# Zero products ahead of TensorE's first work, one pair by product instead of two, fills moved, and weight loads issued a slot earlier, in an attention and hard-swish kernel

## The chip, the cores and the metric

The kernel runs on one core of a Trainium2 chip. The metric is device time in microseconds (us) of one execution. The profile is of one such execution, and times in it count from its start. TensorE (PE, with its weight loads PEld), VectorE (DVE), ScalarE (ACT), GpSimd (POOL) and SyncE (SP) each run their own list of instructions in order and wait for each other on semaphores; transfers go through queues that SP, ACT and POOL feed.

## The reference

Attention over 8 batches of 8 heads, with 576 positions and 64 columns a head, then a two-layer network over all 4608 tokens:

```python
scores = matmul(q, k.T) / 8
cum = cumsum(maximum(s, 0))
scores = where(causal, -1e9, scores + minimum(-(cum[i] - cum[j]), 0))
attn = softmax(scores)
x = (attn @ v)                    # heads side by side: 4608 x 512
h = x @ w_in                      # 512 -> 2048
out = (h * clip(h + 3, 0, 6) / 6) @ w_out   # 2048 -> 512
```

The bias `cum[j] - cum[i]` is a product of rows: the kernel gets it inside the score product by giving q and k a few more rows.

## The kernel before

**Pairs.** The 64 heads are worked as 32 pairs, p = 0 to 31; four pairs (`PPB`) are one batch. For a pair, q and k come in as float32, are cast to float16 tokens `tok`, transposed by TensorE into `qk` (64 rows for the numbers, rows 64 to 67 for the bias), and v is cast into `va`, whose columns 64 and 65 hold ones so that the product with P also gives the sum of the softmax. Each head has three score banks (`scores(p, hh, 0..2)`, then one `corner` a pair), an exponential on ACT into `P`, and fifteen products with `va` (`av`, line 372). `norm` divides, and `transpose_x` puts the pair's result into `xT`, which the network reads.

**The bias.** `load_aug` (line 137) copies rows of the running sum into rows 64 to 67 of `qk` by DMA. In the first pairs, `p < NROW` (two of them before), this copy would come late; there rows 64 to 67 are filled with zeros, and the bias comes by separate products of 128 rows (`by_rows`, line 268, and line 313) from `rows_of` and `picked`, a masked copy of the sums for each head (line 622).

**The front.** `s` is loaded, DVE takes its running sum (lines 593 to 619: scale, scan, and four steps that split it in float16 parts), ACT casts the first pair's tokens, PE transposes them (line 219), and DVE and ACT copy the transposes into `qk` (line 205). Before the running sum DVE works through a row of fills (lines 567 to 589).

**The order by hand.** All instructions stand in an order written out in the loop over p. For p below 4 only attention runs. From p = 4 on `group()` puts a piece of the network between the steps of attention, by turns four products of the first layer (`m1`, line 438, into `ph`) and four of the second (`m2`, line 465, into `po`); pieces become due by counts, whatever the data's arrival, so PE meets a late weight by standing still. Up to p = 8 only the first batch's pieces are due, so these slots have fewer of them.

**Loads.** SP issues v and, for the first four pairs and from pair 9, q and k (lines 114, 125, 129). POOL issues the tokens of pairs 4 to 8 with a cast on the way (line 109), the bias rows, and the weights: `w_in` in four pieces (I0 to I3, line 145), `w_out` in eight (U0 to U7, line 153), each in the slot of the pair that `weights_in` names. Being in order, POOL issues none of them while it waits: it casts q, k and v, and `load_aug` waits there until PE has done the scores that still read the rows to be overwritten.

Of the kernel before, what the change touches and what calls it, by code (L numbers as in the profile page):

```python
# [9 lines left out]
F32 = mybir.dt.float32  # L10
F16 = mybir.dt.float16
# [7 lines left out]
def kernel(  # L19
# [10 lines left out]
    nc = tc.nc  # L30

    B, H, SEQ, D = q.shape
# [5 lines left out]
    NP = NHEADS // 2  # L38
    PPB = H // 2
# [5 lines left out]
    NQK = 3  # L45
    NRAW = 3
    VW = 66
    NROW = 2

# [16 lines left out]
    def keep(name, shape, dt, n=1):  # L68
        made = [
            cpool.tile(shape, dt, name=f"{name}{i}", tag=f"{name}{i}") for i in range(n)  # L70
        ]
        return made if n > 1 else made[0]
# [17 lines left out]
    bias3 = keep("bias3", [128, 1], F32)  # L90
    rows_of = keep("rows_of", [128, 2, 640], F16, 2)
    sel = keep("sel", [128, 4], F32)
    picked = keep("picked", [128, 4, SEQ], F16)

# [24 lines left out]
    def load_v(p, eng):  # L121
        b, h0 = p // PPB, 2 * (p % PPB)
        vraw = vraws[p % NRAW]
        for hh in range(2):
            eng.dma_start(
                out=vraw[:, hh, 0:4, :],
                in_=v[b, h0 + hh, 0:512, :].rearrange("(t p) d -> p t d", p=128),
            )
        eng.dma_start(
            out=vraw[0:64, :, 4, :],  # L130
            in_=v[b, h0 : h0 + 2, 512:SEQ, :].rearrange("h p d -> p h d"),
        )
# [27 lines left out]
    def fill(eng, ap, value):  # L160

        word = np.array([value, value], np.float16).view(np.float32)[0]
        eng.memset(ap.bitcast(F32), float(word))  # L163

    def init_va(i, eng):


        fill(eng, vas[i][:, :, 0:4, 64:66], 1.0)
        fill(eng, vas[i][0:64, :, 4, 64:66], 1.0)
        fill(eng, vas[i][64:128, :, 4, :], 0.0)  # L170
# [41 lines left out]
    def transpose(p, i, copies=(nc.vector.tensor_copy, nc.vector.tensor_copy)):  # L212
        tok, qk = toks[p], qks[p % NQK]
        pt = t_bank(i == 1, "pt")
        if flat(p):
            for c in range(5):
                w = 128 if c < 4 else 64
                c0 = 9 * D * i + 128 * c
                nc.tensor.transpose(  # L219
                    pt[0:w, 128 * c : 128 * (c + 1)], tok[:, c0 : c0 + w], ident  # L220
                )
            order(qk, i, pt.rearrange("p (t c) -> p t c", c=128), 0, copies)
            return
        for hh in range(2):
            for c in range(3):
                n = 96 * (3 * hh + c)
                nc.tensor.transpose(
                    pt[:, n : n + 96],
                    tok[:, i, hh, 2 * c : 2 * c + 2, :].rearrange("p e d -> p (e d)"),
                    ident[0:96, 0:96],  # L230
                )
        on_act = i == 1 and p % 2 == 0
        copies = (nc.scalar.copy if i else nc.vector.tensor_copy,
                  nc.scalar.copy if on_act else nc.vector.tensor_copy)
        for par in range(2):
            to = qk[0:64, 0, i, par : par + SEQ]
            copies[par](
                out=bass.AP(
                    to.tensor,
                    to.offset,  # L240
                    [list(to.ap[0]), [2 * SPAD + 64, 2], [6, 96], [2, 3]],
                ),
                in_=pt[64 * par : 64 * par + 64, 0:SEQ].rearrange(
                    "p (h c t) -> p h t c", h=2, c=3
                ),
            )
# [282 lines left out]
    for p in (1, 2):  # L529
        for i in range(2):  # L530
            load_qk(p, i)
        load_v(p - 1, nc.sync)
    fill(nc.gpsimd, ident, 0.0)
    nc.gpsimd.affine_select(
        out=ident,
# [21 lines left out]
    def set_stair(i, copy):  # L557
        for hh in range(2):
# [4 lines left out]
                in_=stair_sb[64:128, :, None, :].to_broadcast([64, 2, 5, 128]),  # L563
            )

    ones = work.tile([128, SEQ], F32, tag="ones", bufs=1)
    nc.vector.memset(ones, 1.0)
    nc.vector.memset(bias3, 3.0)
    fill(nc.gpsimd, rows_of[0][:, 0, :], 1.0)
    fill(nc.gpsimd, rows_of[0][:, 1, SEQ:640], 0.0)  # L570
    for i in range(NROW):
        fill(nc.vector, qks[i][64:68, :, :, :], 0.0)
    for i in range(NQK):
        init_va(i, nc.gpsimd)
    for i in range(NQK):
        for hh in range(2):
            r = SEQ + 64 * hh
# [43 lines left out]
    def pick(g):  # L621
        nc.vector.tensor_scalar(
            out=picked[:, g, :],
            in0=rows_of[0][:, 0, 0:SEQ],
            scalar1=sel[:, g : g + 1],
            scalar2=None,
            op0=ALU.mult,
        )
# [13 lines left out]
    pick(0)  # L642
    transpose(0, 0)
    transpose(0, 1, (nc.scalar.copy,) * 2)
    for g in range(1, 2 * NROW):
        pick(g)
    cast_qk(1)
    cast_v(0)
    load_aug(2, nc.sync)
    cast_qk(2)  # L650
    for i in range(2):
        load_qk(4, i)
    cast_v(1)
    nc.sync.dma_start(out=stair_sb, in_=stair_dram.ap())


    I, U = load_w_in, load_w_out
    weights_in = {
        3: ((I, 1),),
        4: ((U, 0), (U, 1)),  # L660
        5: ((I, 2), (U, 2)),
        6: ((U, 3), (I, 3)),
        7: ((U, 4), (U, 5)),
        8: ((U, 6), (U, 7)),
    }
    for p in range(NP):
        nxt = p + 1 < NP
        if p + 3 < NP:
            load_v(p + 3, nc.sync)
        if NPE <= p + 4 < NP:  # L670
            for i in range(2):
                load_qk(p + 4, i)
        if p == 2:
            load_w_in(0)
        if PPB <= p < PPB + 3:
            set_stair((p + 1) % NQK, nc.gpsimd.tensor_copy)
            load_aug(p + 1, nc.gpsimd)
        if p and p < NP - 2 and not PPB <= p + 1 < PPB + 3:
            load_aug(p + 2, nc.gpsimd)
        c = p + 2  # L680
        if p and c < NP and flat(c):
            cast_qk(c)
            if c >= NPE:
                crossbar_qk(c)
        if p and nxt:
            cast_v(p + 1)
        for fn, c in weights_in.get(p, ()):
            fn(c)
        if 2 <= p and p + 3 < NPE:
            for i in range(2):  # L690
                load_qk(p + 3, i)
        if p == 10:
            load_s(1, (nc.sync,) * 4)
            fill(nc.gpsimd, rows_of[1][:, 0, :], 1.0)
        if p == 11:
            cum1(1, nc.gpsimd)
        if p == 12:
            cum2(1)
            nc.gpsimd.tensor_copy(out=rows_of[1][0:32, 0, 0:SEQ], in_=C["c"][0:32])
        if p == 13:  # L700
            cum3(1, nc.gpsimd)
            cum4(1, nc.gpsimd)
        if p == 13:
            cum5(1, nc.gpsimd)
            cum6(1, nc.gpsimd)

        def get(i):
            if p + 1 < NPE:
                transpose(p + 1, i)
            elif nxt:  # L710
                spread(p + 1, i)

        if p < PPB:
            scores(p, 0, 0)
            scores(p, 0, 1)
            get(0)
            scores(p, 0, 2)
            corner(p)
            if p:
                av(p - 1, 1, 0)  # L720
                av(p - 1, 1, 1)
                norm(p - 1, 1)
            get(1)
            scores(p, 1, 0)
            scores(p, 1, 1)
            if p:
                transpose_x(p - 1)
            av(p, 0, 0)
            scores(p, 1, 2)
            av(p, 0, 1)  # L730
            norm(p, 0)
            continue

        if p == PPB:
            early[0] = False
            scores(p, 0, 0)
            av(p - 1, 1, 0)
            m1_begin(0, 0, NKC - 1)
            av(p - 1, 1, 1)
            norm(p - 1, 1)  # L740
            scores(p, 0, 1)
            m1_begin(0, 1, NKC - 1)
            transpose_x(p - 1)
            group()
            group()
            scores(p, 0, 2)
            get(0)
            nc.vector.tensor_scalar(
                out=masks, in0=shut, scalar1=65504.0, scalar2=None, op0=ALU.add
            )  # L750
        else:
            scores(p, 0, 0)
            get(0)
            group()
            scores(p, 0, 1)
            av(p - 1, 1, 0)
            group()
            scores(p, 0, 2)
            av(p - 1, 1, 1)
            norm(p - 1, 1)  # L760
            group()
        corner(p)
        group()
        if p > NPE:
            x_done[0] = p - 1
        scores(p, 1, 0)
        get(1)
        group()
        scores(p, 1, 1)
        av(p, 0, 0)  # L770
        if p > PPB:
            (crossbar_x if p >= NPE else transpose_x)(p - 1)
        group()
        scores(p, 1, 2)
        group()
        av(p, 0, 1)
        norm(p, 0)
        group()
# [40 lines left out]
```

## Time and profile before

| What | Value |
|---|---|
| Time, median of 3 runs | 374.91 us (374.88 to 375.51) |
| Span of the profiled execution | 375.0 us |
| PE busy | 348.3 us, 93% |
| PEld, DVE, ACT, POOL busy | 52%, 66%, 59%, 34% |
| Start of pair 0, 1, 2, 3 on PE (first score product) | 8.28, 20.14, 26.01, 30.10 us |
| Start of pair 4, 5, 6, 7, 8, 9, 10 | 34.69, 43.42, 53.22, 63.30, 77.81, 83.29, 89.40 us |
| Moved by DMA | 52.74 MB, 141 GB/s on average |

The first table row is the metric. The starts of the pairs were read from PE's timeline; they show how long the front and each slot of the loop take, and a change in the front or in the weights must show as a shift of these starts. In a busy figure of PE a matmul counts until its modelled end, so a PE that is 100% busy can still be a slow one: the length of one 128x512 product (0.38 us or 0.61 us) tells at which clock it ran.

### The profile page before, as it was taken

What the parts mean: (1) busy time and instruction counts of PE and PEld (TensorE: products, weight loads), DVE (VectorE), ACT (ScalarE), POOL (GpSimd) and SP (SyncE); (2) the same over time, 40 slices, a digit from 0 to 9 for tenths busy, and PEclk for the clock granted to TensorE, in tenths of its full rate; (3) what the DMA queues carried; (4) which work ended last, traced back from release to release, by engine and by line L of the source; (5) the groups of instructions that cost most, each with busy time, mean ns of one, the idle gap of its engine ahead of it and who ended that gap; (6) DMA issues with size and microseconds to landing.
All of it is one profiled execution on the core that took longest, in us unless ns stands there. A gap on an engine that the chain in (4) does not pass through costs nothing.

```text
span 375.0 us, 7741 instructions
## 1 busy us (share of the span) xinstructions
PE 348.3 (93%) x2884; PEld 193.2 (52%) x2884; DVE 247.4 (66%) x545; ACT 220.4 (59%) x382; POOL 127.4 (34%) x231
## 2 busy tenths in 40 slices
PE   2799888588999899999999999999999999999995
PEld 1576555354555455555555555555555544444442
DVE  8657877457689977767668676767676635545541
ACT  4368876466667566666666666666666443443420
POOL 4669974072364943333333333333300000000000
PEclk9999999899999999999999999999999999999999
DMA  9999999949989688989898899797721201101102
GB/s 184 218 154 192 214 202 192 172 77 216 178 207 174 119 201 162 213 148 181 173 186 174 192 163 200 156 190 163 118 60 40 67 1 58 56 0 58 57 29 83
DMA packets 158157, 52.74 MB, mean 141 GB/s; under 512 B 146864, under 2 KB 153024, under 8 KB 158120
## 3 DMA queue, kind: packets, MB, share of 16 engines
q1 hardware_dynamic: 148632, 45.60, 61.2%
q0 software_dynamic: 8224, 6.21, 10.4%
q10 hardware_dynamic: 1264, 0.44, 0.6%
q8 instruction: 22, 0.36, 0.4%
q14 instruction: 15, 0.12, 0.1%
HBM read 37.36 MB, written 9.44 MB: 125 GB/s over the span
## 4 chain that ended last, share of the span: by engine, by line
PE 79%; DMA 10%; DVE 5%; POOL 3%; issue 2%; ACT 0%; POOLq 0%; DVEq 0%
PE po L465 31%; PE ph L438 29%; PE S L302 6%; PE O L372 6%; DMA w_out_sb<-in_moe_w_out_dram 5%; PE S L291 3%; DMA vraw<-in_v_dram 2%; DMA w_in_sb<-in_moe_w_in_dram 2%; DVE qk L205 1%; POOL va L181 1%; DVE qk L163 1%; PE S L313 1%; PE pt L219 1%; POOL tok L177 1%; DVE P L323 0%
## 5 line engine op out<-in xcount | busy, mean ns | idle before, releaser
L454 DVE SCALAR_TENSOR_TENSOR gT<-tr,ph 128x512 f16<-128x512 f32 x144 | 98.6, 685 | 85.9 <-ACT tr L453 84.8
L465 PE MATMUL po<-w_out_sb,gT 128*128 128x512 f16 x576 | 146.9, 379 | 7.4 <-DMA w_out_sb<-in_moe_w_out_dram 6.1
L438 PE MATMUL ph<-xT,w_in_sb 128*128 128x512 f16 x576 | 149.0, 380 | 1.0 <-DVE xT L414 0.5
L321 ACT ACTIVATE P<-S 128x512 f16<-128x512 f32 x192 | 112.1, 595 | 57.1 <-PE S L291 28.7
L453 ACT ACTIVATE tr<-ph,bias 128x512 f32<-128x512 f32 x144 | 99.0, 688 | 78.5 <-PE ph L438 69.0
L137 POOL DMA_DIRECT2D qk<-rows_of x58 | 33.7, 582 | 132.5 <-PE S L302 73.6
L465 PEld LDWEIGHTS <-gT 128*128 128x128 f16 x576 | 49.8, 97 | 53.6 <-issue 7.3
L438 PEld LDWEIGHTS <-w_in_sb 128*128 128x128 f16 x576 | 51.7, 98 | 44.5 <-issue 1.1
L302 PE MATMUL S<-qk 68*128 68x448 f16 (+3 forms) x256 | 50.3, 278 | 0.8 <-ACT P L321 0.8
L372 PE MATMUL O<-va,P 128*128 128x65 f16 x896 | 48.6, 194 | 0.9 <-DVE x L395 0.9
L372 PEld LDWEIGHTS <-P 128*128 128x128 f16 x896 | 40.2, 98 | 15.4 <-DVE x L395 1.5
L302 PEld LDWEIGHTS <-qk 68*128 68x128 f16 x256 | 24.2, 100 | 26.1 <-issue 2.4
L205 DVE COPY qk<-jt 64x768 f16<-64x768 f16 x92 | 33.4, 363 | 4.5 <-DMA jt<-tok 3.1
L177 POOL CAST tok<-raw 128x576 f16<-128x576 f32 x52 | 34.0, 686 | 1.1 <-DMA raw<-in_k_dram 0.6
L395 DVE TENSOR_TENSOR x<-O,rl 128x320 f16<-128x320 f32 x64 | 31.5, 492 | 2.2
L474 DVE TENSOR_SCALAR ob<-po 128x512 f32<-128x512 f32 x36 | 24.6, 684 | 7.4 <-PE po L465 7.4
L291 PEld LDWEIGHTS <-qk 128*128 128x128 f16 (+1 forms) x256 | 19.7, 99 | 16.2 <-issue 2.5
L291 PE MATMUL S<-qk 128*128 128x128 f16 (+1 forms) x256 | 25.5, 221 | 1.9 <-DVE qk L205 1.2
L323 DVE TENSOR_TENSOR P<-P,masks_sb 128x512 f16<-128x512 f16 x54 | 23.7, 439 | 4.2 <-ACT P L321 4.1
L181 POOL CAST va<-vraw 128x512 f16<-128x512 f32 x32 | 20.2, 631 | 2.6 <-issue 1.9
L394 DVE RECIPROCAL rl<-O 128x5 f32<-128x5 f32 x64 | 12.1, 188 | 7.0 <-PE O L372 6.9
L372 PE MATMUL O<-va,PC 128*128 128x65 f16 x64 | 12.4, 194 | 0.0
(66 smaller groups left out, 165.7 us busy)
## 6 DMA issues: line engine op xcount, KB each, us to landing
out_dram<-ob SPq DMA_DIRECT2D x36, 256.0 KB, 2.1
vraw<-in_v_dram SPq DMA_DIRECT2D x64, 128.0 KB, 3.0
raw<-in_q_dram SPq DMA_DIRECT2D x27, 288.0 KB, 3.9
raw<-in_k_dram SPq DMA_DIRECT2D x26, 288.0 KB, 6.7
w_in_sb<-in_moe_w_in_dram POOLq DMA_DIRECT2D x4, 512.0 KB, 7.8
w_out_sb<-in_moe_w_out_dram POOLq DMA_DIRECT2D x8, 256.0 KB, 6.6
vraw<-in_v_dram SPq DMA_DIRECT2D x32, 32.0 KB, 2.7
qk<-rows_of POOLq DMA_DIRECT2D x58, 9.0 KB, 3.5
```

The lines of the kernel that those rows point to most:

```text
L137: eng.dma_start(out=qks[p % NQK][64:68, hh, :, 64 * hh : 64 * hh + SEQ], in_=rows_of[g // 32].rearrange("(r g) i t -> g r i t", g=32)[g % ...
L177: copy(out=toks[p][:, c], in_=raws[p % NRAW][:, c])
L205: copies[par](out=qk[0:64, :, i, 128 * par : 128 * par + 256 * n].rearrange("p h (s two c) -> p h s two c", two=2, c=128)[:, :, :, 0, :], ...
L291: mm(S[:, c], lhsT=kT[rows, c], rhs=qT[rows, c], start=(j == 0 and not by_product), stop=(j == 3),)
L302: mm(S[:, c : c + w], lhsT=kT[0:68, 128 * j : 128 * (j + 1)], rhs=qT[0:68, 128 * (j + 1) : SEQ], start=(c == 0), stop=(c != 0 and p >= NROW),)
L321: nc.scalar.activation(out=pt[:, c], in_=S, func=AF.Exp, scale=0.125)
L372: mm(o[:, i, :], lhsT=lhsT, rhs=va[:, hh, j, 0:65], **kw)
L395: nc.vector.tensor_tensor(out=X[p][:, :, hh, :], in0=o[:, :, 0:64], in1=rl.to_broadcast([128, 5, 64]), op=ALU.mult,)
L438: mm(ph, lhsT=w_in_sb[:, kc, ft * 128 : (ft + 1) * 128], rhs=xT[:, kc, n * 512 : (n + 1) * 512], start=(kc == 0), stop=(kc == NKC - 1),)
L453: nc.scalar.activation(out=tr, in_=ph, func=AF.Relu, bias=bias3[:, 0:1])
L454: nc.vector.scalar_tensor_tensor(out=gTs[n][:, ft, :], in0=tr, scalar=6.0, in1=ph, op0=ALU.min, op1=ALU.mult)
L465: mm(po, lhsT=gTs[n][:, ft, t4 * 128 : (t4 + 1) * 128], rhs=w_out_sb[:, ft, :], start=(ft == 0), stop=(ft == NFT - 1),)
```

## The change

It aims at PE's clock and waits in the first 90 us.

- `NROW` goes from 2 to 1: only pair 0 takes its bias by products. Pair 1 gets it by `load_aug(1)`. The zero fill of `qk[0]` rows moves from DVE to the head of POOL, that of `qk[1]` goes, and two of four `picked` rows go.
- A tile of zeros (128x512, the head of `xT`) is filled first thing on DVE, and PE multiplies it 22 times before its first transposes and 4 times after them (`NWARM`), all into one PSUM buffer ("o", one buffer). The results aren't read.
- The fills of `va` move from POOL to DVE.
- `load_aug(1)` and `load_aug(2)` go to POOL, ahead of the casts of pair 1 and of v 0; in the loop `load_aug` moves behind the casts.
- I0 is issued in the front in place of slot 2, I1 and I2 one slot sooner, I3 two, and U2 to U7 one slot sooner (U3 too); U0 and U1 stay in slot 4. The tokens of pair 4 and the `stair_sb` load leave the front for slot 1.

```diff
-    NROW = 2
+    NROW = 1
+    NWARM = (22, 4)
...
-    picked = keep("picked", [128, 4, SEQ], F16)
+    picked = keep("picked", [128, 2, SEQ], F16)
...
+    for i in range(NROW):
+        fill(nc.gpsimd, qks[i][64:68, :, :, :], 0.0)
     fill(nc.gpsimd, ident, 0.0)
...
+    fill(nc.vector, xT[:, 0, 0:512], 0.0)
+
+    def warm(n):
+        for _ in range(n):
+            W = psum.tile([128, 512], F32, tag="o", name="W")
+            nc.tensor.matmul(
+                W, lhsT=xT[:, 0, 0:128], rhs=xT[:, 0, 0:512], start=True, stop=True
+            )
+
+    warm(NWARM[0])
     ones = work.tile([128, SEQ], F32, tag="ones", bufs=1)
     nc.vector.memset(ones, 1.0)
+    for i in range(NQK):
+        init_va(i, nc.vector)
...
-    for i in range(NROW):
-        fill(nc.vector, qks[i][64:68, :, :, :], 0.0)
-    for i in range(NQK):
-        init_va(i, nc.gpsimd)
...
     transpose(0, 1, (nc.scalar.copy,) * 2)
+    warm(NWARM[1])
     for g in range(1, 2 * NROW):
         pick(g)
+    load_aug(1, nc.gpsimd)
     cast_qk(1)
+    load_aug(2, nc.gpsimd)
     cast_v(0)
-    load_aug(2, nc.sync)
     cast_qk(2)
-    for i in range(2):
-        load_qk(4, i)
+    load_w_in(0)
     cast_v(1)
-    nc.sync.dma_start(out=stair_sb, in_=stair_dram.ap())
...
-        3: ((I, 1),),
-        4: ((U, 0), (U, 1)),
-        5: ((I, 2), (U, 2)),
-        6: ((U, 3), (I, 3)),
-        7: ((U, 4), (U, 5)),
-        8: ((U, 6), (U, 7)),
+        2: ((I, 1),),
+        3: ((I, 2),),
+        4: ((I, 3), (U, 0), (U, 1)),
+        5: ((U, 2), (U, 3)),
+        6: ((U, 4), (U, 5)),
+        7: ((U, 6), (U, 7)),
...
+        if p == 1:
+            nc.sync.dma_start(out=stair_sb, in_=stair_dram.ap())
...
-        if p == 2:
-            load_w_in(0)
...
-        if p and p < NP - 2 and not PPB <= p + 1 < PPB + 3:
-            load_aug(p + 2, nc.gpsimd)
         c = p + 2
...
             cast_v(p + 1)
+        if p and p < NP - 2 and not PPB <= p + 1 < PPB + 3:
+            load_aug(p + 2, nc.gpsimd)
...
-        if 2 <= p and p + 3 < NPE:
+        if p and PPB <= p + 3 < NPE:
             for i in range(2):
                 load_qk(p + 3, i)
```

## Prediction

> **What bounds the kernel now.** I read the page's slices first, then PE's waits, then PE's timeline where those waits lie. The page:
>
> ```profile
> PE   2799888588999899999999999999999999999995
> DVE  8657877457689977767668676767676635545541
> PEclk9999999899999999999999999999999999999999
> GB/s 184 218 154 192 214 202 192 172 77 216 178 207 174 119 201 162 213 148 181 173 186 174 192 163 200 156 190 163 118 60 40 67 1 58 56 0 58 57 29 83
> ```
>
> A slice is 9.4 us. From slice 11 on PE is full until the end, so whatever is saved before some 90 us should come off the end, one for one; all that the change touches lies before that. PE's waits:
>
> ```profile
> PE pt L219 <- ACT tok L177: 6.7, 1, 6.7
> PE po L465 <- DMA w_out_sb<-in_moe_w_out_dram: 6.1, 4, 2.9
> PE S L268 <- DVE picked L622: 2.6, 1, 2.6
> PE po L465 <- DVE x L395: 1.2, 1, 1.2
> ```
>
> Of 26.7 us without PE work (375.0 - 348.3), 6.7 are the wait for the first tokens, 2.6 for the running sum, 6.1 for pieces of w_out. Busy PE isn't fast PE, though. PE's timeline, columns start, length, work:
>
> ```profile
> 16.34 0.61 PE L284 MATMUL S<-shut,ident 128*128 128x512 f16 x1
> 20.14 0.62 PE L284 MATMUL S<-shut,ident 128*128 128x512 f16 x1
> 26.01 0.38 PE L284 MATMUL S<-shut,ident 128*128 128x512 f16 x1
> 70.18 0.59 PE L465 MATMUL po<-w_out_sb,gT 128*128 128x512 f16 x2 [2.93 <-DMA w_out_sb<-in_moe_w_out_dram]
> 71.96 0.87 PE L465 MATMUL po<-w_out_sb,gT 128*128 128x512 f16 x2 [1.19 <-DMA w_out_sb<-in_moe_w_out_dram]
> ```
>
> The same product takes 0.61 us until 20.9 us (the products at 20.97 are short) and 0.38 later: pair 0, 8.28 to 20.14, ran entirely at half clock. The wait at 70 us costs twice, for in the windows after it the clock (the last but two column) is down:
>
> ```profile
> 72.50:73.00 0.50, 0.50 (x3) 0.15 (x2) 0.00 (x0) 0.00 (x0) 0.00 (x0) 0.50 1.26 252
> 75.50:76.00 0.50, 0.50 (x5) 0.28 (x3) 0.00 (x0) 0.15 (x1) 0.00 (x0) 0.94 0.00 0
> ```
>
> At the front that column says 1.00 while products are slow, so there I go by the lengths.
>
> [...] the reduced shares of windows 72.00:72.50 (0.64) and 75.50:76.00 (0.94) put the slow stretch at 72.14 to 75.56, 3.42 us[...] the trace has 0.61 and 0.38 as lengths, while undisturbed starts lie 0.40 to 0.43 apart slow and 0.22 fast (four products of L438 in 0.86).
>
> **The change, part by part.**
>
> *Zero products.* In the built program each waits on TensorE's own semaphore for the one before, as all write one PSUM buffer. So I take the length, not the start distance: about 0.65 us slow and 0.43 fast (0.61 and 0.38 plus 0.04 to 0.05, an estimate from DVE's step of 0.03 between dependent rows at 23.62). The floor is 0.43 and 0.22. DVE starts at 0.93; the zero tile is 256 of the 576 elements that take 0.54, so 0.24; PE starts near 1.3. [...] say 6.9: (6.9 - 1.3)/0.65 = 8.6 slow, 13.4 x 0.43 = 5.8 fast, end 12.7. All of PE is queued behind: the transposes, ready from 6.7 before, now run 12.7 to 13.6; behind them ACT's copies of k (1.40, to 15.0), DVE's of q (0.99, to 14.3), and the four later products (1.7, to 15.3). Pair 0 then needs, fast, about 8,850 columns / 2.4 = 3.7 us, 0.8 for fifteen products of `av` and 0.3 of gaps: 15.3 + 4.8 = **20.1, against 20.14**. What the clock gives, the queue of zeros takes. Pair 1's first 0.83 us also was slow: -0.4.
>
> *Fills.* Off DVE go two rows of 1.34; on come 0.24 and nine small fills at 0.08 (six of a kind took 0.48), 0.7. The scale step at 5.70 can start when s has landed, issue to 1.6 plus up to 3.1, about 4.2. `picked` is done near 9.9, not 11.5: 1.6 us, but hidden under the zeros until 12.7: 0. It counts only in the rival with short products. The fill on POOL (some 1.7 us from 0.36 for 320 elements) delays `ident` to about 2.9, needed at 12.7: 0. Fewer `picked` rows (two at 0.42) are off the path.
>
> *Pair 1 without products by rows.* Gone are 2 x 3 sets of 512 columns and 128 of the corner: 6 x 0.22 + 0.06 = **-1.4**. `load_aug(1)` waits on POOL for the sums (about 9.1) and takes 1.2; behind it the casts of pair 1 end at 12.1, which PE wants near 16.5; the rows land near 14, wanted at 20: 0.
>
> *Weights.* Before, U4 and U5 stood in slot 7 behind a `load_aug` that waits for PE (POOL idle 5.26 to 61.83), were issued from 64.4 and arrived after PE asked at 67.2. Now they stand in slot 6, where the corresponding place on POOL is 53: landing in 6 to 8 us (the page's 6.6 median), they are in by 61. U3 goes from 53.15 to about 45, wanted at 57.6; U6, U7 from 78.9 to 65, wanted at 86. So the four waits, 1.50 + 2.93 + 1.19 + 0.53 = 6.1, go. The slow stretch goes too: 72.62 to 75.65 is 3.03 for what took 1.62 at 59.52 to 61.14, plus 0.4 on the products at 71.96: 1.8. Against it, DVE and ACT use those waits to catch up (97% busy in 66 to 69), so I give back 1.6: **-6.3**. New: I3 before U0 and U1. They leave POOL near 36 to 37 and land at 43 to 46; PE wants them about 46.5. Transfers are full at 215 GB/s around then, with a gap at 21 to 27 us (108 and 144 GB/s) that I0, now issued near 16, partly fills. 0, up to 1.5.
>
> *Pair 4's tokens* were issued at 14.06; now behind `load_aug(3)`, which waits for pair 0's scores, near 21, landing 7.9 later: about 29, when PE asks for them in pair 3 (28.5 + 0.7). 0, up to 1.
>
> Sum: 0 - 0.4 - 1.4 - 6.3 = -8.1; 374.9 - 8.1 = 366.8, say **367.0**.
>
> **Rivals.**
> - *Short products* (no real wait): 22 end near 8.5, the earlier sum counts, pair 0 ends near 16: -4.1 more. But then pair 3 asks for pair 4's tokens near 25 and waits 2 to 3. Net 365; 363 without that wait. Against it: the semaphore.
> - *Zeros don't raise the clock.* [...] Then 22 x 0.65 = 14.3 ends at 15.6, transposes 17.2, four products 19.8, pair 0 another 8 us slow: 27.8, +7.7; then -1.4, and -7.4 from weights that now are in long before: 374.9 - 1.1 = 373.8.
> - *The same, and the waits for weights only change their name* (for DVE's `x`, ACT's P, as at 48.6): 4 back instead of 7.4: 377, slower.
>
> **How the numbers follow.** Main case 0.55 (367.0, 364 to 369), short products 0.15 (365), slow zeros 0.2 (373.8, 371 to 376), slower rival 0.1 (377). The range 363 to 374.5 leaves out the last case and the upper two fifths of the slow one, about 0.18. Faster by over 0.2% (below 374.2): 0.70 and 0.10 of the slow case, 0.80. Same: 0.06. Slower: 0.14.
>
> **What would show it.** Zero products 0.65 then 0.43 apart, ending near 12.7, first full-clock product by 8; pair 1 starting near 20, pair 2 near 24.3, pair 4 near 32.8; no wait of L465 for w_out; no reduced clock near 72; pair 10 near 81. It's wrong if the zeros stay 0.65 apart to the end (pair 1 near 28), if they lie 0.22 apart (pair 1 near 16), or if w_out still is waited for, meaning that transfers and not their issue were the limit.

## The result

The changed kernel takes **373.35 us** (median of 4, 372.53 to 373.82), the kernel before 374.89 in the same comparison (374.41 to 375.51). The ratio is 0.9955, interval 0.9931 to 0.9979: faster by 0.45%, where 367.0 (2.1%) was forecast.

The two profiles are further apart than the medians: the span went from 375.0 to 370.8 us, since the profiled execution of before took 376.75 us and that of the changed kernel 372.53. So I use the traces to see where time moved, and the medians for how much.

The page of the changed kernel, its slices, and the row of the added products:

```profile
PE   7999888979999999999999999999999999999995
DVE  7158687777689977676767676767675644544531
PEclk9999999999999999999999999999999999999999
...
L574 PE MATMUL W<-xT 128*128 128x512 f16 x26 | 15.2, 585 | 2.6 <-DVE xT L164 1.2
```

PE is busy from the first slice and the low clock of slice 8 is gone. But the mean of the 26 zero products is 585 ns: they are slow (those of the network, L439 of the same page, take 379). PE's timeline of the front (start, length, work):

```profile
1.20 14.05 PE L574 MATMUL W<-xT 128*128 128x512 f16 x22 [1.20 <-DVE xT L164]
15.04 1.66 PE L220 MATMUL pt<-ident,tok 128*128 128x128 f16 x10
16.64 2.53 PE L574 MATMUL W<-xT 128*128 128x512 f16 x4
18.96 0.63 PE L285 MATMUL S<-shut,ident 128*128 128x512 f16 x1
...
20.11 0.38 PE L303 MATMUL S<-qk 68*128 68x448 f16 x2
```

The 22 products lie (14.05 - 0.58) / 21 = 0.64 us apart, to the end. Only at 20 us, under the score products, does work become fast. PE's waits, as before the longest first:

```profile
PE ptx L410 <- DVE qk L238: 1.5, 1, 1.5
PE po L466 <- DVE x L396: 1.2, 1, 1.2
PE W L574 <- DVE xT L164: 1.2, 1, 1.2
```

No wait for w_out is left in the list; all of its 6.1 us are gone. Both can be read from the starts of the pairs (first score product, us). Two entries of the table ahead of the prediction were misread: 89.40 is the second head of pair 9, and pair 10 starts at 93.98; 43.42 is the weight load of pair 5, whose first product starts at 43.45.

| Pair | 0 | 1 | 2 | 3 | 4 | 5 | 6 | 7 | 8 | 9 | 10 |
|---|---|---|---|---|---|---|---|---|---|---|---|
| before | 8.28 | 20.14 | 26.01 | 30.10 | 34.69 | 43.45 | 53.22 | 63.30 | 77.81 | 83.29 | 93.98 |
| changed | 18.96 | 24.18 | 28.27 | 32.36 | 36.96 | 46.05 | 55.81 | 65.88 | 75.27 | 80.75 | 90.75 |
| difference | 10.7 | 4.0 | 2.3 | 2.3 | 2.3 | 2.6 | 2.6 | 2.6 | -2.5 | -2.5 | -3.2 |

The front costs 4.0 us, pair 1 gives 1.8 back, between pairs 7 and 8, where w_out was waited for, 5.1 come off, and between pairs 9 and 10 another 0.7.

A last 1.1 us come off far behind the first 90 us, at which the change aims. The profile before has this wait:

```profile
PE S L291 <- DVE qk L205: 1.2, 2, 1.1
```

Its longer part, 1.06 us at 128.1 us, is gone in the changed kernel. The cause is the place of `load_aug` in the loop, which holds for later pairs too: the seven profiles with `load_aug` ahead of the casts (before and runs 4, 6, 7, 9, 10 and 12 below) all have a wait of 1.05 or 1.06 us at this point, the seven with it behind them (changed and runs 1, 2, 3, 5, 8 and 11) have none, and runs 5 and 6 differ in nothing else.

### The profile page after: what moved, and what is told of

The parts are those of the page before. It is cut to its first block, busy times and chain, and to the rows that moved or that the text cites. A ratio compares the mean times of both kernels' runs of the same rounds, so it can differ in the third digit from the quotient of the medians.

```text
span 370.8 us, 7780 instructions
## 1 busy us (share of the span) xinstructions
PE 355.5 (96%) x2892; PEld 191.8 (52%) x2892; DVE 244.4 (66%) x551; ACT 219.5 (59%) x382; POOL 130.8 (35%) x227
## 4 chain that ended last, share of the span: by engine, by line
PE 88%; DVE 7%; ACT 3%; issue 1%; ACTq 0%
PE po L466 32%; PE ph L439 31%; PE O L373 7%; PE S L303 7%; PE W L574 4%; PE S L292 3%; DVE gT L455 2%; DVE qk L238 2%; ACT tr L454 1%; DVE x L396 1%; PE pt L220 1%; DVE qk L206 1%; DVE P L324 1%; PE ptx L410 1%; ACT P L322 1%
## 5 line engine op out<-in xcount | busy, mean ns | idle before, releaser
L439 PE MATMUL ph<-xT,w_in_sb 128*128 128x512 f16 x576 | 148.2, 379 | 1.2 <-DVE gT L455 0.7
L439 PEld LDWEIGHTS <-w_in_sb 128*128 128x128 f16 x576 | 51.5, 97 | 44.6 <-issue 0.9
L138 POOL DMA_DIRECT2D qk<-rows_of x62 | 36.0, 582 | 72.0 <-PE S L303 61.8
L303 PE MATMUL S<-qk 68*128 68x448 f16 (+3 forms) x256 | 49.1, 272 | 0.8 <-ACT P L322 0.8
L324 DVE TENSOR_TENSOR P<-P,masks_sb 128x512 f16<-128x512 f16 x54 | 24.8, 460 | 4.3 <-ACT P L322 4.3
L574 PE MATMUL W<-xT 128*128 128x512 f16 x26 | 15.2, 585 | 2.6 <-DVE xT L164 1.2
```

The costliest lines, as they stand in the source:

```text
L138: eng.dma_start(out=qks[p % NQK][64:68, hh, :, 64 * hh : 64 * hh + SEQ], in_=rows_of[g // 32].rearrange("(r g) i t -> g r i t", g=32)[g % ...
L303: mm(S[:, c : c + w], lhsT=kT[0:68, 128 * j : 128 * (j + 1)], rhs=qT[0:68, 128 * (j + 1) : SEQ], start=(c == 0), stop=(c != 0 and p >= NROW),)
L439: mm(ph, lhsT=w_in_sb[:, kc, ft * 128 : (ft + 1) * 128], rhs=xT[:, kc, n * 512 : (n + 1) * 512], start=(kc == 0), stop=(kc == NKC - 1),)
```

## Experiments

All times are medians; each ratio is against the kernel before on the same chip. Theory A after the result: the clock stayed low because each zero product waits for the one before; theory B: products over zeros don't raise it. The times at which expectations let the clock rise were the author's estimates.

**1. No wait between the zero products.**

```diff
-        for _ in range(n):
-            W = psum.tile([128, 512], F32, tag="o", name="W")
-            nc.tensor.matmul(
-                W, lhsT=xT[:, 0, 0:128], rhs=xT[:, 0, 0:512], start=True, stop=True
-            )
+        W = psum.tile([128, 512], F32, tag="o", name="W") if n else None
+        for i in range(n):
+            nc.tensor.matmul(
+                W, lhsT=xT[:, 0, 0:128], rhs=xT[:, 0, 0:512],
+                start=(i == 0), stop=(i == n - 1),
+            )
```

> The changed kernel, but the 22 and the 4 products over zeros accumulate in one PSUM group each, so that none waits for the one before (starts 0.43 us apart instead of 0.63). Theory A, the clock stayed low [...] then 0.22 apart; the 22 end near 8.8, pair 1 starts near 16, pair 4 waits some 2 us for its tokens; 365.4 us. Theory B, products over zeros don't count at all: 0.43 apart to the end, ending at 10.7; pair 0 slow, pair 1 near 22; 370 us.

371.48 us, ratio 0.988 (0.9846 to 0.9915). PE's timeline:

```profile
1.20 7.42 PE L574 MATMUL W<-xT 128*128 128x512 f16 x22 [1.20 <-DVE xT L164]
8.45 1.06 PE L220 MATMUL pt<-ident,tok 128*128 128x128 f16 x10
9.45 1.04 PE L574 MATMUL W<-xT 128*128 128x512 f16 x4
10.32 0.38 PE L285 MATMUL S<-shut,ident 128*128 128x512 f16 x1
...
27.84 0.66 PE L228 MATMUL pt<-ident,tok 96*128 96x96 f16 x6 [2.23 <-DMA tok<-in_q_dram]
...
49.24 0.59 PE L466 MATMUL po<-w_out_sb,gT 128*128 128x512 f16 x2 [1.04 <-DMA w_out_sb<-in_moe_w_out_dram]
```

The same 22 products over the same zeros now take 7.42 us. With 0.43 apart slow and 0.216 fast, 21 intervals in 7.04 us mean about 12 slow ones: the clock rose near 6.3, an estimate from these lengths. Theory A holds at the front: without waits the same zeros raise the clock. Pair 1 starts at 15.25, 8.9 us sooner than in the changed kernel. But only 2 to 3 us reach the end (2.5 against run 2, on the same chip), and the expected 365.4 was 6 us too low. The later rows say where it goes: PE waits for the tokens of pair 4, then for w_out, and around the first of these waits the clock falls as well. Rows of 3 us of this run, the clock in the last column but two:

```profile
24.00:27.00 3.00, 0.60 (x6) 0.35 (x6) 0.37 (x1) 1.18 (x3) 3.00 (x6) 0.96 0.81 154
27.00:30.00 3.00, 2.16 (x29) 2.04 (x30) 1.45 (x2) 0.77 (x2) 3.00 (x7) 0.50 1.21 205
30.00:33.00 3.00, 3.00 (x30) 2.38 (x28) 1.30 (x4) 2.48 (x4) 2.96 (x5) 0.50 1.19 177
33.00:36.00 3.00, 3.00 (x37) 1.79 (x36) 1.37 (x4) 1.91 (x4) 2.96 (x5) 0.90 1.25 205
```

**2. Ones in place of zeros**, still waiting for each other.

```diff
-    fill(nc.vector, xT[:, 0, 0:512], 0.0)
+    fill(nc.vector, xT[:, 0, 0:512], 1.0)
```

> The changed kernel with the tile filled with 1.0 instead of 0.0, products still waiting for each other. Theory A (waits): no difference, 0.63 us apart to the end, pair 1 near 24.2, 373.4 us. Theory B (zeros don't count): the clock rises by 8 us, the 22 end near 12.7, pair 1 near 20, 368 us.

373.98 us, 0.9957 (0.9932 to 0.9982), and the row of the 22 is that of the zeros to the hundredth:

```profile
1.20 14.05 PE L574 MATMUL W<-xT 128*128 128x512 f16 x22 [1.20 <-DVE xT L164]
```

Between the values zero and one there is no difference; theory B falls.

**3. No added products.**

```diff
-    NWARM = (22, 4)
+    NWARM = (0, 0)
-    fill(nc.vector, xT[:, 0, 0:512], 0.0)
```

> The changed kernel without any products over zeros and without their tile; all other parts stay. Theory: the products delay PE's first work by some 7.5 us and bring no clock before it: without them score products start near 10, pair 1 near 18.5, pair 2 near 23, no waits for w_out; 366.5 us. Rival, the products help by the clock that they leave for pair 0: without them pair 0 is slow and nothing is won, 373 us or more.

371.26 us, 0.989 (0.985 to 0.993). PE's timeline:

```profile
8.25 0.61 PE L285 MATMUL S<-shut,ident 128*128 128x512 f16 x1
...
16.28 0.63 PE L373 MATMUL O<-va,P 128*128 128x65 f16 x8
16.72 0.48 PE L303 MATMUL S<-qk 68*128 68x320 f16 x2
17.04 0.38 PE L314 MATMUL S<-picked,rows_of 128*128 128x320 f16 x2
```

Pair 0 is slow until some 16.9 us, and then its own work has raised the clock; pair 1 still starts at 17.47, 6.7 sooner than with the waiting products. These cost 2.7 us of the result (373.98 in run 2, on the same chip, against 371.26; the intervals lie just apart). At 366.5 the expectation was 5 us too low: as in run 1, PE waits 2.1 us for pair 4's tokens, and the gain is not passed on.

**4. The order of weight loads alone**, on the kernel before.

```diff
+    load_w_in(0)
     cast_v(1)
...
-        3: ((I, 1),),
-        4: ((U, 0), (U, 1)),
-        5: ((I, 2), (U, 2)),
-        6: ((U, 3), (I, 3)),
-        7: ((U, 4), (U, 5)),
-        8: ((U, 6), (U, 7)),
+        2: ((I, 1),),
+        3: ((I, 2),),
+        4: ((I, 3), (U, 0), (U, 1)),
+        5: ((U, 2), (U, 3)),
+        6: ((U, 4), (U, 5)),
+        7: ((U, 6), (U, 7)),
...
-        if p == 2:
-            load_w_in(0)
```

> The kernel before with the order of weight loads of the changed one alone (first piece of w_in in the front, others as changed). Theory: pairs 0 to 6 start as before, the waits for w_out and the slow stretch near 72 us go, pair 10 some 5.5 us sooner; 369.4 us. Rival, transfers and not their issue were the limit, so waits move to U0 and U1: 373 us or more.

370.50 us, 0.9861 (0.9829 to 0.9893): 5.3 us, more than the whole changed kernel brings. Of the waits for w_out one remains:

```profile
PE po L465 <- DMA w_out_sb<-in_moe_w_out_dram: 0.5, 1, 0.5
```

It is for U1, at 47.48. The waits and the slow stretch go, as the theory said, and the time is 1.1 us above its 369.4; the rival holds in part. Pairs 1 to 5 start some 2 us sooner than in the profile before, though the front is the same: in this execution products are already fast at 19.91 us (0.39 for two score products that take 0.62 at 18.90 in the profile before), and not from 20.9 on. Pair 2 starts at 23.79 instead of 26.01; as slow products start about twice as far apart (0.43 against 0.22), that puts the rise near 16.5, an estimate.

**5. Pair 4's tokens in the front again**, on run 1.

```diff
     cast_qk(2)
+    for i in range(2):
+        load_qk(4, i)
     load_w_in(0)
...
-        if p and PPB <= p + 3 < NPE:
+        if p > 1 and PPB <= p + 3 < NPE:
```

> The changed kernel with the products over zeros in one group each, and the tokens of pair 4 issued in the front again, as in the kernel before. Theory: with them late PE waited 2.2 us in pair 3 [...]; now pair 4 starts near 29 instead of 33.7, and about half of it, 2 to 3 us, reaches the end: 368.7 us. Rival, transfers set the pace until pair 6 (w_out and tokens land no sooner than 49 us, whenever PE is there): pair 4 is earlier, pair 7 still near 63.5, 371 us.

372.25 us, 0.9908 (0.9884 to 0.9932). The wait for tokens is gone, and pair 3 waits for its bias rows instead, so pair 4 starts at 31.80, not 29:

```profile
26.69 0.38 PE L292 MATMUL S<-qk 68*128 68x128 f16 x4 [3.08 <-DMA qk<-rows_of]
...
48.58 0.66 PE L466 MATMUL po<-w_out_sb,gT 128*128 128x512 f16 x2 [0.75 <-DMA w_out_sb<-in_moe_w_out_dram]
```

The theory is refuted. The rival is supported: pair 7 starts at 64.50, no sooner than in run 1 (63.59).

**6. `load_aug` ahead of the casts in the loop as well**, on run 5.

```diff
+        if p and p < NP - 2 and not PPB <= p + 1 < PPB + 3:
+            load_aug(p + 2, nc.gpsimd)
         c = p + 2
...
             cast_v(p + 1)
-        if p and p < NP - 2 and not PPB <= p + 1 < PPB + 3:
-            load_aug(p + 2, nc.gpsimd)
```

> The run before this one, and load_aug ahead of the casts again in the loop, as in the kernel before. Theory: the 1.2 us that pair 3 waited for its bias rows (behind a cast that waits for v) go, pair 3 starts near 23.7, 1 us less at the end at most: 368 us. Rival: the wait only moves to v, no difference to the run before.

371.05 us, 0.9882 (0.9857 to 0.9906). Pair 3's wait fell from 3.08 to 1.20 us, pair 4 starts at 29.85, and pair 5 then waits 2.77 us for its own bias rows and starts at 41.83, as in runs 1 and 5 (42.21, 42.10). Pair 7 starts at 62.64, 1.9 us ahead of run 5, but the wait of 1.05 us described under the result is back, at 122.8. Whether this run is faster than run 5 the intervals leave open.

**7. Weights as in run 4, zero products in one group each (`warm` as in run 1), the rest as before.**

```diff
+    fill(nc.vector, xT[:, 0, 0:512], 0.0)
+    warm(22)
...
     transpose(0, 1, (nc.scalar.copy,) * 2)
+    warm(4)
```

> The kernel before with the changed order of weight loads (as in the run of the weights alone) and with 22 and 4 products over zeros in one group each; front, tokens and pairs by product as before. Theory: the clock is up near 7 us, pair 1 starts near 16.5 instead of 18.8, pair 4 near 30.5; if that reaches the end, 368.5 us. Rival, transfers set the pace: pair 7 at 62, 370.5 us as with the weights alone.

370.59 us, 0.9872 (0.9846 to 0.9898): what run 4 gave without them. Pair 1 starts at 16.90 (18.31 in run 4), pair 4 at 31.06 (32.47), pair 5 at 41.18 (41.21). So the 1.4 us are gone by pair 5, whose first product waited 1.25 us. The trace names DVE's `x`, which this product doesn't read; its bias rows, issued at 33.2 and 33.8 and 7.4 to 7.8 us on the way, land at about that time and are the likelier cause, which no run shows. After that the first work on w_out waits, 2.4 us here and 0.5 in run 4:

```profile
46.38 0.59 PE L465 MATMUL po<-w_out_sb,gT 128*128 128x512 f16 x2 [1.32 <-DMA w_out_sb<-in_moe_w_out_dram]
48.09 0.59 PE L465 MATMUL po<-w_out_sb,gT 128*128 128x512 f16 x2 [1.12 <-DMA w_out_sb<-in_moe_w_out_dram]
```

**8. Zero products in groups of two**, else the changed kernel: does a wait at every second product keep the clock low too?

```diff
-        for _ in range(n):
-            W = psum.tile([128, 512], F32, tag="o", name="W")
+        for i in range(n):
+            if i % 2 == 0:
+                W = psum.tile([128, 512], F32, tag="o", name="W")
             nc.tensor.matmul(
-                W, lhsT=xT[:, 0, 0:128], rhs=xT[:, 0, 0:512], start=True, stop=True
+                W, lhsT=xT[:, 0, 0:128], rhs=xT[:, 0, 0:512],
+                start=(i % 2 == 0), stop=(i % 2 == 1),
             )
```

> The changed kernel with its products over zeros in groups of two: the second doesn't wait for the first, the third waits for the second. Two take 0.43 + 0.63 us, so they stream 81% of the time instead of 68%. Theory, [...] the clock rises by 8 us, the 22 end near 9.5. Rival, any wait for the own semaphore keeps the clock down: slow to the end, 22 in 11.7 us, end near 12.9.

One execution, 372.02 us. The row of the 22:

```profile
1.20 8.50 PE L575 MATMUL W<-xT 128*128 128x512 f16 x22 [1.20 <-DVE xT L164]
```

8.50 us, not 11.7: counted as in run 1, with groups 1.07 us apart slow and 0.65 fast (estimates from the spacings above), the clock rose near 4.8, with a wait at every second product. So it isn't the wait as such: with one at every product, 0.64 us apart, the clock stayed low for 14.05 us.

In runs 1 and 3 to 8, whatever the front, PE got U1 between 47.5 and 49.2 us, with pair 1 starting anywhere from 15.0 to 18.3. GpSimd issued U0 and U1 at much the same time in all of them, from 35.9 to 37.6 us on, so this alone doesn't tell whether issue or transfer set the time. Two profiles do: before, with I2 and I3 behind them, they left at 36.00 and took 6.4 and 7.4 us; in run 4, with I2 and I3 ahead, they left at 35.90 and took 9.9 and 10.8. With I2 and I3 ahead of it U1 took 3.4 us longer. The next run changes the order.

**9. U0 and U1 ahead of I2 and I3**, on run 7.

```diff
-        3: ((I, 2),),
-        4: ((I, 3), (U, 0), (U, 1)),
-        5: ((U, 2), (U, 3)),
+        3: ((U, 0), (U, 1)),
+        4: ((I, 2), (U, 2)),
+        5: ((U, 3), (I, 3)),
```

> The kernel before with products over zeros in one group each, and the changed order of weights but U0 and U1 one slot sooner, ahead of I2 and I3 (slot 3: U0, U1; slot 4: I2, U2; slot 5: U3, I3). Theory, in all runs so far the first products of the second layer got U1 near 48 us because everything issued before it takes that long to move: with about 1 MB less ahead, U0 and U1 are in near 43, the waits of 1.3 and 1.1 us in pair 5 go, pair 7 starts near 60.5, 368.8 us. Rival, pair 5 is held by other waits (DVE's x, the bias rows): 370.5 us as before.

**368.13 us, 0.9797 (0.9784 to 0.981)**, the best of all. No wait for w_out is left; the first of its products waits for DVE only:

```profile
45.46 1.04 PE L465 MATMUL po<-w_out_sb,gT 128*128 128x512 f16 x4 [0.64 <-DVE x L395]
```

Pairs 1 to 4 start as in run 7, pair 5 0.2 sooner, pair 6 2.2 and pair 7 2.6 sooner, at 60.18. The order up to U1 set the pace. Two things change with it, and this run doesn't separate them: U0 and U1 are issued 7.1 us sooner than in run 7 (28.88 against 36.00), and take 7.3 and 9.2 us, not 10.2 and 11.3. Without zero products, or with `load_aug` behind the casts, this order was not run.

**10. The same order on run 6, I0 in slot 1.**

```diff
-    load_w_in(0)
...
         2: ((I, 1),),
-        3: ((I, 2),),
-        4: ((I, 3), (U, 0), (U, 1)),
-        5: ((U, 2), (U, 3)),
+        1: ((I, 0),),
+        3: ((U, 0), (U, 1)),
+        4: ((I, 2), (U, 2)),
+        5: ((U, 3), (I, 3)),
```

> The changed kernel with products over zeros in one group each, pair 4's tokens in the front, load_aug ahead of the casts, and the weights as in the run beside this, with I0 in slot 1. Theory: the bias rows of pair 3 no longer queue behind I0, its wait of 1.2 us goes and pair 4 starts near 28.8; U0 and U1 come near 43: 368.5 us. Rival, transfers of q, k, v alone set the pace of pairs 1 to 4 (4.1 us a pair): 371 us.

369.52 us, 0.9845 (0.9824 to 0.9865). Pair 3 no longer waits for bias rows and pair 4 starts at 27.88, 3.2 us ahead of run 9. But pair 4 now waits 1.29 us for its rows, and pair 5 1.68, and starts at 41.29, behind run 9's 40.95. The wait moved; the gain did not pass, and the time is 1.0 above the theory's 368.5.

**11. The change's other parts alone**: run 3 (no zero products) with the weights ordered as before.

```diff
-    load_w_in(0)
...
-        2: ((I, 1),),
-        3: ((I, 2),),
-        4: ((I, 3), (U, 0), (U, 1)),
...
+        3: ((I, 1),),
+        4: ((U, 0), (U, 1)),
+        5: ((I, 2), (U, 2)),
...
+        if p == 2:
+            load_w_in(0)
```

> The changed kernel without products over zeros and with the order of weight loads of the kernel before: what is left is one pair by product, the moved fills, the bias rows on GpSimd and the late tokens of pair 4. Theory, an earlier front alone meets the same transfers: pair 1 some 2 us earlier, but the waits for w_out grow by as much, pair 10 as before: 375.5 us. Rival, it is worth what it shows at pair 1: 373 us.

374.10 us, 0.9965 (0.9948 to 0.9981). Pair 1 starts at 16.58, 3.6 us sooner than in the profile before; U4 and U5 are waited for again:

```profile
PE po L466 <- DMA w_out_sb<-in_moe_w_out_dram: 2.3, 2, 1.2
PE S L292 <- DMA qk<-rows_of: 2.3, 1, 2.3
```

Neither expectation: these parts are worth 1.3 us, between the two. Two things go into it that neither named. From the wait for bias rows on, products are slow until some 42 us, and the wait of 1.06 us that `load_aug`'s place removes is gone. The slow stretch in PE's timeline (the same four products at 28.30 and 41.12):

```profile
28.30 0.39 PE L292 MATMUL S<-qk 68*128 68x128 f16 x4
...
33.26 0.60 PE L292 MATMUL S<-qk 68*128 68x128 f16 x4 [2.32 <-DMA qk<-rows_of]
...
41.12 0.63 PE L292 MATMUL S<-qk 68*128 68x128 f16 x4
```

**12. The moved fills**, on run 9.

```diff
-    for i in range(NROW):
-        fill(nc.vector, qks[i][64:68, :, :, :], 0.0)
-    for i in range(NQK):
-        init_va(i, nc.gpsimd)
+    for i in range(NROW):
+        fill(nc.gpsimd, qks[i][64:68, :, :, :], 0.0)
+    for i in range(NQK):
+        init_va(i, nc.vector)
```

> The best run so far (kernel before, products over zeros in one group each, weights sooner with U0 and U1 ahead of I2 and I3) with the moved fills as well: both zero fills of qk rows at the head of GpSimd, those of va on VectorE. Theory: the running sum is ready 1.6 us sooner, pair 1 starts near 15.8 and pair 4 near 29.7 (17.35 and 31.28 without); DMA waits in pairs 3 to 5 take most of it back, 367.6 us. Rival, it passes to the end, 366.6 us.

369.34 us, 0.9842 (0.9813 to 0.9871): no gain on run 9, and if anything a loss. The intervals just miss each other, on different chips, and single executions went from 367.96 to 371.61. Neither expectation came true. Pair 1 starts at 15.49 and pair 5 at 40.87, against 16.91 and 40.95: bias rows are waited for 0.48 us in pair 2 and 1.48 in pair 5. 1.4 us at pair 1 became 0.1 at pair 5.

## Why the prediction was wrong

- **The step that failed: the clock rises under the zero products.** The forecast let the clock rise near 6.9 under products that wait for each other, the author's estimate, which no trace of before shows, and so the 22 end at 12.7. (Its 2.4 columns a ns for fast products are four of L438, 2,048 columns, in 0.86 us.) Their slow spacing was right (0.65 said, 0.64 measured), but the clock rose only at 20 us, under the score products. The 22 ended at 15.25, pair 0 started at 18.96 (15.3 said) and pair 1 at 24.18 (20.1 said): 4.0 us lost by a term put at 0. Run 2 shows that the zeros aren't to blame, and runs 1 and 8 that closer zero products do raise the clock.
- **The trace spoke against it.** The forecast let zero products raise the clock in 5.6 us (1.3 to 6.9). In the profile before PE works without a gap from the end of its last wait, at 12.44, and stays slow for another 8.5 us, until 20.9:

```profile
12.44 0.48 PE L291 MATMUL S<-qk 68*128 68x128 f16 x3 [0.19 <-DVE qk L205]
...
20.55 0.58 PE L268 MATMUL S<-picked,rows_of 128*128 128x128 f16 x4
20.97 0.22 PE L291 MATMUL S<-qk 68*128 68x128 f16 x1
```

PE busy for 5.6 us hadn't been enough there.

- **The rival "zeros don't raise the clock"** had the event and the time (373.8), though not the reason in its name. The time was in part luck, as two terms were off in opposite directions: it let pair 1 start at 27.8, and the clock rose in time for 24.18; and its 7.4 us from weights were 5.8 (5.1 between pairs 7 and 8 and 0.7 between pairs 9 and 10).
- **Pair 1 without products by rows:** 1.4 and 0.4 said; from pair 1 to pair 2 the shift went from +4.0 to +2.3, which is 1.8 before rounding. Right.
- **Fills:** the running sum was to be ready near 9.9, hidden behind the zeros. `picked` was done at 8.99, 2.5 us sooner than before, and DVE then waited 6.97 us for the transposes. Hidden, as said.
- **Weights:** said -6.3; all four waits and the slow stretch near 72 us went, and DVE waits of 1.5 and ACT waits of 0.6 came, where 1.6 had been given back. -5.8 in the trace, -5.3 by run 4. Right to a microsecond. GpSimd's timeline shows U4 and U5 leaving at 57.0, while the forecast had 53; PE wanted them at 69.9:

```profile
57.00 1.49 POOL L154 DMA_DIRECT2D w_out_sb<-in_moe_w_out_dram  x2
```

- **U0 and U1 behind I3,** put at 0 to 1.5, cost nothing here because PE was late (its first product on w_out started at 51.16). In each run with an earlier front and this order they cost: from 0.4 in run 6 to 2.8 in run 8. **Pair 4's tokens,** 0 to 1, cost nothing either for the same reason, and 2.1 to 2.6 in runs 1, 3 and 8, in runs 1 and 8 with a fall of the clock (four score products take 0.63 us at 30.66 and 30.47, and 0.39 in run 3 at 30.18).
- **That all time saved before some 90 us comes off the end** was too simple. Runs 1 and 3, 2.2 us apart at pair 1, start pairs 7 to 10 within 0.02 us of each other. So it doesn't hold for what is saved in the front, ahead of a stage that transfers pace. The trace showed this stage: 183 to 241 GB/s from 27 to 54 us, and the prediction used it only to bound a single wait. Nor does all of the change lie before 90 us: the 1.1 us of `load_aug`'s place were left out.

In the profiles these steps make up the 4.2 us between the spans to within 0.2. Of them 2.7 are missing in the medians (1.5), and why stays open. The start of the fast clock differs between executions: 20.9 in the profile before, near 16.5 by the estimate in run 4, whose front is the same. That would make pair 0 shorter or longer by some 2 us, but no trace of other executions of the kernel before shows it.

## What to carry to other kernels

Products meant only to raise TensorE's clock did so here when they stood close together: 22 accumulated in one PSUM group took 7.42 us, with the clock up near 6.3 (run 1). With one buffer rewritten each time, each waited for the one before, 0.64 us apart, and the clock stayed low for all 14.05 us. Even the close ones brought nothing at the end (run 7 against run 4), for another stage came behind them. Before shortening a front, look for the stage behind it that transfers pace; there, order the loads by when they are wanted. Here one slot's swap in that stage gave 2.5 us (run 9 over run 7), while 3.1 us won at pair 1 gave nothing (run 1 against run 4).

## What the runs showed of the hardware

- **Zero products and the clock.** 22 products of 128x512, each waiting for the one before, lay 0.64 us apart and stayed slow for all 14.05 us, over zeros (changed kernel) and over ones (run 2). In groups of two they took 8.50 us (run 8, one execution) and in one group 7.42 (run 1), and by the estimates given there the clock rose near 4.8 and near 6.3. Zeros raised it, so what was multiplied needn't have been real data.
- **Without zero products** PE worked without a gap for 8.5 us in the profile before (12.44 to 20.9) and for 6.9 in run 3 (10.01 to 16.9) before its products became fast. What the clock counts was not shown.
- **The clock also fell when PE was partly idle.** In run 1 PE worked 0.60 us from 24 to 27, between waits of 1.20 and 2.23, and by the rows there the clock was at 0.50 from about 26.8 to 33.6 us. In the profile before it fell after a stretch with 0.63 us of work:

```profile
66.00:69.00 3.00, 1.25 (x13) 0.77 (x12) 2.94 (x7) 2.97 (x7) 0.61 (x1) 1.00 0.96 136
69.00:72.00 3.00, 0.63 (x3) 0.23 (x3) 0.20 (x1) 0.33 (x1) 0.00 (x0) 1.00 1.23 228
72.00:75.00 3.00, 3.00 (x20) 1.81 (x20) 0.46 (x1) 0.60 (x1) 0.00 (x0) 0.52 0.76 147
```

The first of these rows, with 1.25 us of work, left it at 1.00, and so did 1.47 us of work from 45 to 48 in run 1. How long one wait is didn't decide it: after 2.06 us in run 3 products stayed fast (0.38 at 28.81), after 2.23 us in run 1 they were slow (0.63 at 28.30).
